# Attention and MLP in fp32 on one core: the MLP as two groups of four batches, with 26 products of sums for each matrix product

## The chip, the core and the metric

The kernel runs on one core of one Trainium2 chip. The core has five engines with instruction streams of their own: TensorE (PE in the profile, with its weight loads as PEld), VectorE (DVE), ScalarE (ACT), GpSimd (POOL, unused here) and SyncE (SP), which issues all transfers between DRAM and the on-chip memory SBUF; 16 DMA engines carry them out. PE writes its results to PSUM, from where DVE or ACT takes them. The metric is the device time of one execution in microseconds. Before the change it was 1048.71 us, the median of three runs from 1046.14 to 1048.9.

## The reference

Sigmoid attention over 8 batches with 12 heads of 448 rows and 64 columns, and behind it an MLP over all 3,584 rows, all in fp32:

```python
scores = scale * np.matmul(q, k.transpose(0, 1, 3, 2)) - np.log(S)
attn = 1.0 / (1.0 + np.exp(-scores))
attn_out = np.matmul(attn, v)                      # 8 x 12 x 448 x 64
x = attn_out.transpose(0, 2, 1, 3).reshape(B * S, H * D)   # 3584 x 768
h = x @ w_in                                       # 768 x 2048
g = h * (1.0 / (1.0 + np.exp(-1.702 * h)))
out = g @ w_out                                    # 2048 x 768
```

The MLP's weights arrive in double precision and are decoded to fp32 on the chip.

## The kernel before

**Precision.** An fp32 operand of the MLP is split into a rounded part and the rest. A matrix product of two operands is three matmuls (high x low, low x high, high x high), added up in PSUM (`TERMS`, function `matmuls`, L819). A split is a rounding copy on ACT or DVE (hi) and a subtraction on DVE (lo): L782, L783 and L785 for weights, L1033, L1034 and L1045 for x and g.

**Attention.** For each pair of heads: scores on PE (L598, L614 for the rows that are left over), a sigmoid on ACT (L584), the product with v on PE (L629, L642), a copy to SBUF (L666, L667) and a store to DRAM (`spill`, named xd). Meanwhile the 16 weight blocks are decoded, DVE and ACT taking turns (L504 to L527), and some of them are stored to DRAM (f).

**MLP.** The 3,584 rows are cut into seven blocks of 512 (`T`). Block 0 is computed directly (`first_block`): 576 matmuls. The other six are two triples (`triple`). For a triple, w_in is 8 blocks (4 x 2) and x is 6 blocks (2 x 3), and in place of the 24 products of blocks it forms 20 products of *sums* of weight blocks with *sums* of x blocks (`W_SUMS`, `X_SUMS`), from which the 12 blocks of h are added up (`H_SUMS`); the same for w_out, g and the output (`G_SUMS`, `O_SUMS`). One product is 36 matmuls in four parts (three parts in the second layer); its result fills four (three) banks of PSUM, and two such places, h0 and h1, take turns. The result is copied (L1178, L1179) or added (L1212) into SBUF, or a later product adds onto it in PSUM (chains, and seeds, which ACT copies into PSUM first, L1135 and L1137).

Sums of weights are formed once (L762; `sums_ahead` and, in the first triple, `w_sums`), split, and stored split in DRAM (c). Later uses load them from there (w<-c). A weight sum has two halves (h = 0 and 1), each a tile of 768 KB, and the ring `wsplit` has four of these tiles. Splits of x or g lie in the ring `pair`, which has two.

**What sets the order.** `Plan.run` places all tasks by a list of keys and estimated costs, and writes each engine's stream in that order. PE's order in the MLP is `SEQUENCES`. Streams are in order: an instruction that waits holds up all behind it on its engine, on SP as well. Buffers for sums are slots of three sizes (`SLOTS`), some of which open only when attention has ended (`LATE_SLOTS`).

Of the kernel before, what the change touches and what calls it, by code (L numbers as in the profile page):

```python
# [20 lines left out]
T = 512  # L21
# [16 lines left out]
ATTENTION, LATE = ("qk", "vraw", "a", "al", "raw64", "e", "qkraw", "x32"), ("wsplit",)  # L38
# [44 lines left out]
class Apart:  # L83
# [216 lines left out]
class Sums:  # L300


    def __init__(self, ops, uses, leaf, cost, make, fresh):
        self.ops = {o[0]: o[1:] for o in ops}
        self.leaf, self.cost, self.make, self.fresh = leaf, cost, make, fresh
        self.left, self.nodes = {}, {}
        for _, a, b, _ in ops:
            for v in (a, b):
                self.left[v] = self.left.get(v, 0) + 1
        for v in uses:  # L310
            self.left[v] = self.left.get(v, 0) + 1

    def get(self, v):
        if v in self.nodes:
            return self.nodes[v]
        if v not in self.ops:
            self.nodes[v] = self.leaf(v)
            return self.nodes[v]
# [15 lines left out]
        self.nodes[v] = Node(into, view, [t])  # L334
        return self.nodes[v]
# [3 lines left out]
def sigmoid_attention_mlp(ctx: ExitStack, tc: tile.TileContext, qk, v, w, out):  # L339
# [62 lines left out]
    def make(b, tag, shape, dtype, name):  # L402
        late = tag in LATE or tag == b.slot and int(tag[1:]) >= EARLY_SLOTS[tag[0]]
# [11 lines left out]
        if b.apart:  # L415
            psum[tag].close()
            banks("z", "left" if tag == "h0" else "right")
            b.tile = Apart([
                spaces["z"].tile([P, T], dtype, tag=f"z{i}", name=f"{name}_{i}", bufs=1) for i in range(NJ)
            ])  # L420
            return b.tile
# [31 lines left out]
    def round_and_rest(costs, b, src, deps, uses, hi, lo, first=lambda: None):  # L453
# [7 lines left out]
        else:  # L461
# [13 lines left out]
    combined = [[[dram.tile([P, 2 * NW_EL], F32, name=f"c{m}_{r}_{h}", tag=f"c{m}_{r}_{h}") for h in range(2)]  # L475
                 for r in range(len(PRODUCTS))] for m in range(2)]
# [4 lines left out]
    def decode(n):  # L481
# [48 lines left out]
        decoded[n] = [Node(f, held(f, f"w32_{n}", NW_EL, k * NW_EL), [t_p]) for k in range(2)]  # L530
        if n >= NW // 4:
# [3 lines left out]
    xs = {}  # L535
# [113 lines left out]
    def places(b):  # L649

        cut = (T - S) * b
        if cut:
            yield b - 1, slice(T - cut, T), slice(0, cut)
        if cut < S:
            yield b, slice(0, S - cut), slice(cut, S)

    copies = []

    def to_x(b, p, t, ps):
# [9 lines left out]
        for block, into, cols in places(b):  # L669
            for js in ([slice(0, 2)] if p % NJ < NJ - 1 else [slice(0, 1), slice(1, 2)]):  # L670
                k, j = divmod(p + js.start, NJ)
                n = js.stop - js.start
                d = dma(lambda block=block, into=into, k=k, j=j, n=n: spill[block][k][:, j : j + n, into],
                        lambda cols=cols, js=js: xb.tile[:, js, cols], n * P * (cols.stop - cols.start) * 4 / 1024, [c], [xb])
                for i in range(n):
                    spilled.setdefault((block, p + js.start + i), []).append(d)

    def make_x(block, k):
        x = buffer("pair")
        n = NJ * T  # L680

        def first():
            if x.tile is None:
                make(x, "pair", [P, 2, 4, T], F32R, f"x{block}_{k}")

        t = [dma(lambda j=j: x.tile[:, 1, j].bitcast(F32), lambda j=j: spill[block][k][:, j], P * T * 4 / 1024,
                 spilled[block, k * NJ + j], [x], first) for j in range(NJ)]
        xs[block, k] = (round_and_rest(
            (act(n), cast(n), dve(n)), x, lambda: x.tile[:, 1, :NJ].bitcast(F32), t, [],
            lambda: x.tile[:, 0, :NJ], lambda: x.tile[:, 1, :NJ],  # L690
        ), x)

# [65 lines left out]
    FULL, PIECE, XB, GB = slice(0, N2), NW_EL, NJ * T, 4 * T  # L758
# [17 lines left out]
    def used_as(block):  # L776
        return [r for r, v in enumerate(W_USES) if v == block]
# [549 lines left out]
```

## Time and profile before

| What | Value |
|---|---|
| Three runs | 1048.9, 1048.71, 1046.14 us |
| The profiled execution | 1047.47 us, its span 1045.5 us |
| Granted TensorE clock | 1.00 |
| HBM | 185.60 MB read, 84.93 MB written |
| DMA queue of SP | 114,640 packets, 270.57 MB, 74.0% of 16 engines |
| L819, first layer's products (p<-xp,w) | 1,440 matmuls, 328.6 us busy |
| L819, second layer's products (p<-gp,w) | 1,440 matmuls, 328.6 us busy |
| L819, block 0 (h<-x,w and o_q<-g,w) | 576 matmuls, 133.0 us busy |

The span is the time from the first to the last instruction on the core; the execution's time is a little longer. Busy times of an engine are united, so overlapping instructions count once. Names in a row are tiles, output first: xp and gp are split sums of x and g, w a split weight block or sum, p a product in PSUM, h and o sums of products, c and f weights in DRAM.

### The profile page before, as it was taken

The numbers are of one execution on the slowest core, as the hardware profiler recorded it, in microseconds if no ns is written. First come the engines' busy times: TensorE is split into PE (matmuls) and PEld (weight loads), VectorE is DVE, ScalarE is ACT, GpSimd is POOL, SyncE is SP. The second block draws the span as 40 slices with busy tenths as digits, with TensorE's granted clock in tenths as the row PEclk, the third lists the DMA queues.
The fourth block names the chain that finished last, engine by engine and source line by source line (L and its number), as shares of the span: only waits on it lengthen the run. The fifth ranks groups of instructions, "written<-read, shape, count | busy, mean of one in ns | idle before, by whom it ended". The sixth has DMA issues, their size and how long they took to land.

```text
span 1045.5 us, 13568 instructions
## 1 busy us (share of the span) xinstructions
PE 1036.4 (99%) x5300; PEld 779.4 (75%) x5300; DVE 852.2 (82%) x758; ACT 543.0 (52%) x497; POOL 0.2 (0%) x4
## 2 busy tenths in 40 slices
PE   9999999999999999999999999999999999999998
PEld 5545555555888877888887888888888888788886
DVE  6999999882998758788998989999874596888685
ACT  6878888875655432533554444333443263534342
POOL 0000000000000000000000000000000000000000
PEclk9999999999999999999999999999999999999999
DMA  9999998973999998756656666859766545454666
GB/s 348 371 362 395 336 397 297 324 258 127 345 332 369 363 377 299 254 193 225 212 170 227 223 210 189 294 200 368 273 232 199 192 139 192 135 167 152 213 201 219
DMA packets 114703, 271.43 MB, mean 260 GB/s; under 512 B 10320, under 2 KB 80080, under 8 KB 112592
## 3 DMA queue, kind: packets, MB, share of 16 engines
q1 hardware_dynamic: 114640, 270.57, 74.0%
q8 instruction: 42, 0.69, 0.3%
q14 instruction: 21, 0.17, 0.0%
HBM read 185.60 MB, written 84.93 MB: 259 GB/s over the span
## 4 chain that ended last, share of the span: by engine, by line
PE 90%; DVE 4%; DMA 2%; ACT 2%; issue 1%; SPq 0%; DVEq 0%; ACTq 0%
PE p L819 55%; PE av L629 11%; PE sc L598 9%; PE h L819 6%; PE o_q L819 5%; PE sc L614 2%; PE av L642 2%; DMA w<-c 1%; DVE gp L1045 1%; DVE h L762 1%; ACT gp L1033 1%; ACT o L1178 1%; DVE o L1179 1%; DMA qkraw<-qk 0%; DVE gs L762 0%
## 5 line engine op out<-in xcount | busy, mean ns | idle before, releaser
L819 PE MATMUL p<-xp,w 128*128 128x512 f32 x1440 | 328.6, 389 | 2.9 <-DMA w<-c 1.2
L819 PE MATMUL p<-gp,w 128*128 128x512 f32 x1440 | 328.6, 389 | 1.1 <-DVE gp L1045 1.1
L819 PEld LDWEIGHTS p<-xp,w 128*128 128x128 f32 x1440 | 270.0, 188 | 60.4 <-issue 2.3
L819 PEld LDWEIGHTS p<-gp,w 128*128 128x128 f32 x1440 | 270.0, 188 | 58.4 <-DVE gp L1045 1.9
L584 ACT ACTIVATE a<-sc,bias 128x896 f32<-128x896 f32 x168 | 156.1, 1017 | 46.1 <-PE sc L614 30.2
L629 PE MATMUL av<-a,vraw 128*64 128x448 f32 x576 | 113.5, 543 | 0.0
L598 PEld LDWEIGHTS sc<-qk 64*128 64x128 f32 x846 | 75.8, 184 | 26.7 <-PE sc L614 16.2
L598 PE MATMUL sc<-qk 64*128 64x448 f32 x846 | 94.3, 373 | 0.3 <-DVE qk L469 0.3
L629 PEld LDWEIGHTS av<-a,vraw 128*64 128x64 f32 x576 | 39.2, 137 | 63.2 <-issue 45.5
L1178 ACT COPY h<-p 128x2048 f32<-128x2048 f32 x18 | 33.7, 1874 | 91.4 <-PE p L819 62.0
L1045 DVE TENSOR_TENSOR gp<-h,gp 128x2048 fp32r<-128x2048 f32 x31 | 70.9, 2288 | 9.1 <-ACT gp L1033 8.7
L1033 ACT CAST gp<-h 128x2048 fp32r<-128x2048 f32 x23 | 44.0, 1912 | 44.8 <-PE p L819 37.5
L819 PE MATMUL h<-x,w 128*128 128x512 f32 x288 | 66.6, 389 | 0.0
L819 PE MATMUL o_q<-g,w 128*128 128x512 f32 x288 | 66.4, 389 | 0.0
L1212 DVE TENSOR_TENSOR h<-h,p 128x2048 f32<-128x2048 f32 x23 | 52.1, 2284 | 17.5 <-PE p L819 10.3
L819 PEld LDWEIGHTS h<-x,w 128*128 128x128 f32 x288 | 54.0, 188 | 11.9 <-issue 0.7
L819 PEld LDWEIGHTS o_q<-g,w 128*128 128x128 f32 x288 | 54.1, 188 | 11.2
L1178 ACT COPY o<-p 128x1536 f32<-128x1536 f32 x18 | 25.9, 1443 | 59.6 <-PE p L819 19.2
L762 DVE TENSOR_TENSOR h<-h,h 128x2048 f32<-128x2048 f32 x24 | 54.7, 2285 | 0.1
L782 ACT CAST wc<-ws 128x384 fp32r<-128x384 f32 (+1 forms) x51 | 28.3, 582 | 47.0 <-DVE ws L762 23.7
L1045 DVE TENSOR_TENSOR xp<-x,xp 128x1536 fp32r<-128x1536 f32 x22 | 38.6, 1754 | 16.6 <-ACT xp L1033 16.5
L1033 ACT CAST xp<-x 128x1536 fp32r<-128x1536 f32 x19 | 28.1, 1481 | 43.6 <-PE p L819 31.5
(108 smaller groups left out, 984.8 us busy)
## 6 DMA issues: line engine op xcount, KB each, us to landing
w<-c SPq DMA_DIRECT2D x140, 384.0 KB, 4.2
w<-c SPq DMA_DIRECT2D x52, 768.0 KB, 4.7
w<-w SPq DMA_DIRECT2D x16, 1536.0 KB, 9.7
c<-wc SPq DMA_DIRECT2D x56, 384.0 KB, 5.3
qkraw<-qk SPq DMA_DIRECT2D x47, 448.0 KB, 6.9
vraw<-v SPq DMA_DIRECT2D x24, 448.0 KB, 8.4
c<-wc SPq DMA_DIRECT2D x14, 768.0 KB, 4.9
c<-w SPq DMA_DIRECT2D x28, 384.0 KB, 4.2
```

The lines of the kernel that those rows point to most:

```text
L584: nc.scalar.activation(a.tile, ps.tile[:, :, :S], AF.Sigmoid, bias=bias, scale=scale)
L598: nc.tensor.matmul(ps.tile[:, j, :S], lhsT=src[kk][rows, S + c * P : S + (c + 1) * P], rhs=src[qq][rows, :S], start=i == 0, stop=i == len( ...
L614: nc.tensor.matmul(ps.tile[cols, j, :S], lhsT=src.tile[rows, S + NC * P :], rhs=src.tile[rows, :S], start=True, stop=True, skip_group_chec ...
L629: nc.tensor.matmul(ps.tile[cols, n % 2, :S], lhsT=vr.tile[:, at : at + D], rhs=a.tile[:, j], start=c == 0, stop=False, skip_group_check=True,)
L642: nc.tensor.matmul(ps.tile[cols, k, :S], lhsT=vr.tile[rows, at : at + D], rhs=a.tile[rows, j], start=False, stop=True, skip_group_check=True,)
L762: return task("DVE", cost, lambda: nc.vector.tensor_tensor(out(), x(), y(), op=op), deps, uses)
L782: t_hi = on_either((act(n), lambda: nc.scalar.copy(into()[:, 0], node.view())), (cast(n), lambda: nc.vector.tensor_copy(into()[:, 0], node ...
L819: nc.tensor.matmul(ps, lhsT=ws[:, a, c * P : (c + 1) * P], rhs=x[:, d, k], start=start and i == 0 and j == 0, stop=stop and i == len(todo) ...
L1033: t_hi = on_either((act(n), lambda: nc.scalar.copy(part(0)(), node.view())), (cast(n), lambda: nc.vector.tensor_copy(part(0)(), node.view())),
L1045: nc.vector.tensor_tensor(part(1)(), node.view(), part(0)().bitcast(F32), op=ALU.subtract)
L1178: t = on_either((act(self.n), lambda: nc.scalar.copy(view(), node.view())), (dve(self.n), lambda: nc.vector.tensor_copy(view(), node.view())),
L1212: nc.vector.tensor_tensor(view(), x.view(), y.view(), op=ALU.add if s0 == s else ALU.subtract)
```

## The change

T becomes 448, so that a block of rows is a batch. The MLP is two groups of four batches (`ROWS = 4`); `first_block` and `triple` go. For a group, w_in is 8 blocks and x is 8 (2 x 4), and the 32 products of blocks are 26 products of sums; likewise in the second layer. There are 104 products of 36 matmuls of 448 columns. New tables say which sums; they have 18 sums of weights (14 before), 18 of x (12), 28 of g (16). One list, `SEQUENCE`, orders the products of both groups and layers; its entries are (group, layer, product).

A weight block is whole now, 1536 columns, and a split one is one tile of 1536 KB in the ring `raw64`, which has two and which the decoding uses earlier; `wsplit` goes. A weight sum is made at its first use, split and stored split (c), and later uses load it.

New is `Sums.used` with `KEEP_FOR`: a sum (or a block) whose next use is further off in the sequence than its number says goes back to DRAM (kw, kx, kg; blocks of x and w_out are there already) and is loaded again. All blocks of g of group 0 are stored when they are made (`AWAY_G`) and loaded for their uses (gl).

```diff
-T = 512
+T = 448
+ROWS = 4
...
-    pair=2, wsplit=4, q0=1, q1=1, q2=1, q3=1, h0=1, h1=1, z=1,
+    pair=2, q0=1, q1=1, q2=1, q3=1, h0=1, h1=1, z=1,
 )
-SLOTS = dict(s=1536, g=2048, t=384)
-EARLY_SLOTS, LATE_SLOTS = dict(s=7, g=4, t=0), dict(s=0, g=9, t=13)
+SLOTS = dict(s=1536, g=1792)
+EARLY_SLOTS, LATE_SLOTS = dict(s=12, g=0), dict(s=2, g=12)
...
+AWAY_G = (0,)
+
+SEQUENCE = (
+    (0, 0, 12), (0, 0, 18), (0, 0, 8), (0, 0, 17), (0, 0, 6), (0, 0, 9), (0, 0, 24), (0, 0, 25),
...
+KEEP_FOR = dict(
+    w0={1: 3, 3: 6, 5: 3, 7: 6, 8: 3, 9: 6, 10: 6, 11: 6, 12: 25, 13: 6, 14: 3, 16: 12, 17: 25, 19: 3, 20: 3, 21: 3, 22: 12, 23: 3, 24: 25, 25: 3},
...
+    def used(self, v):
+
+        turns = self.turns[v]
+        turns.pop(0)
+        if self.left[v] > 0 and turns and turns[0] - self.now > self.keep_for.get(v, math.inf):
+            node = self.nodes.pop(v)
+            if v not in self.back:
+                self.back[v] = self.put(v, node)
...
-    FULL, PIECE, XB, GB = slice(0, N2), NW_EL, NJ * T, 4 * T
+    PIECE, XB, GB = N2, NJ * T, 4 * T
...
     def weights_ring(name):
-        b = buffer("wsplit")
+        b = buffer("raw64")
...
+        def kept(self, name, shape, node, kind):
+
+            kb = P * math.prod(shape) * 4 / 1024
+            n = math.prod(shape)
+            at = dram.tile([P, *shape], F32, name=name, tag=name)
+            t = dma(lambda: at, node.view, kb, node.done, [node.b])
+            node.readers.append(t)
+            count = [0]
+
+            def again():
+                b = plan.slot(kind)
+                count[0] += 1
+                view = tiled(b, f"{name}_{count[0]}", n)
+                return Node(b, view, [dma(view, lambda: at, kb, [t], [b])])
+
+            return again
...
+        def piece_of(self, q, m, r):
+            v = W_USES[r]
+            self.w_later[m, v] -= 1
+            self.begun.add((m, v))
+            b, into, first = weights_ring(f"w{m}_{q}_{r}")
+            if (m, v) in self.saved:
+                t = dma(lambda: into().bitcast(F32), in_dram(m, v), 4 * KB, [self.saved[m, v]], [b], first)
+            else:
+                sums = self.w[m]
+                node = sums.get(v)
+                sums.left[v] -= W_USES.count(v)
                 t = split_piece(node, PIECE, into, b, first)
+                sums.used(v)
+                if self.w_later[m, v]:
+                    self.saved[m, v] = dma(in_dram(m, v), lambda: into().bitcast(F32), 4 * KB, [t], [b])
+            return t, b, into
...
             for i in range(parts):
+                todo = [(i * NJ + j, j) for j in range(NJ)] if m == 0 else [(c * NJ + i, c) for c in range(4)]
...
+                    matmuls(ps.tile[:, i, :T], weights(), xb.tile, todo, not more, True)
+
+                t = task("PE", 3 * len(todo) * 0.2, emit, [t_x, t_w, *edge], [ps, xb, wb])
```

What this does to the streams is seen at three places. On PE, where attention ends and the MLP begins, before stood the direct products of block 0 (h and o_q in PSUM, x and g split whole, w a half block; nine or six matmuls a row):

```order
L642 MATMUL av46_2689<-a47_3_2633,vraw7_4_2558 64x448 x4
L819 MATMUL h0_0_2712<-x0_0_773,w0_0_0_0_1564 128x512 x9
L819 MATMUL h0_0_2712<-x0_1_934,w0_0_0_1_1588 128x512 x9
L819 MATMUL h0_0_2712<-x0_0_773,w0_0_0_0_1564 128x512 x9
L819 MATMUL h0_0_2712<-x0_1_934,w0_0_0_1_1588 128x512 x9
L819 MATMUL h0_1_2769<-x0_0_773,w0_0_1_0_2747 128x512 x9
```

and now stand products of sums at once (xp0 a sum of group 0's x, w0 of w_in):

```order
L689 MATMUL av46_2679<-a47_3_2615,vraw7_4_2529 64x448 x4
L829 MATMUL p0_0_12_2718<-xp0_15_2682,w0_0_12_2617 128x448 x36
L829 MATMUL p0_0_18_2767<-xp0_4_2700,w0_0_18_2463 128x448 x36
L829 MATMUL p0_0_8_2828<-xp0_11_2813,w0_0_8_2777 128x448 x36
L829 MATMUL p0_0_18_2767<-xp0_17_2855,w0_0_17_2840 128x448 x36
L829 MATMUL p0_0_6_2932<-xp0_10_2908,w0_0_6_2906 128x448 x36
```

Block 0 is gone from PE, and the first product of sums has moved up to the end of attention.

On DVE, in the second layer of the first triple, these rows stood before, which serve the products with gp1_2, gp1_27 and gp1_25 (gp is a split of g, h and gs are sums, o is a result copied, w a half of a product's weights):

```order
L785 TENSOR_TENSOR w1_1_2_1_5344<-wr1_6_5263,w1_1_2_1_5344 128x384
L1045 TENSOR_TENSOR gp1_2_5347<-h1_2_4015,gp1_2_5347 128x2048
L762 TENSOR_TENSOR gs1_3_5380<-h1_0_5209,h1_7_4822 128x2048
L1179 COPY o1_21_5395<-p1_1_10_5326 128x1536
L1045 TENSOR_TENSOR gp1_27_5397<-h1_11_4075,gp1_27_5397 128x2048
L783 CAST w1_1_19_1_5401<-w1_1_19_1_5401 128x768
L785 TENSOR_TENSOR w1_1_19_0_5399<-w1_1_19_0_5399 128x768
L785 TENSOR_TENSOR w1_1_19_1_5401<-w1_1_19_1_5401 128x768
L762 TENSOR_TENSOR h1_1_3894<-gs1_3_5380,h1_1_3894 128x2048
L1034 CAST gp1_25_5453<-h1_1_3894 128x2048
L1045 TENSOR_TENSOR gp1_25_5453<-h1_1_3894,gp1_25_5453 128x2048
```

and now, in the second layer of group 1, for the three products with gp1_16, gp1_10 and gp1_41 (kg and kw sums that come back from DRAM, wf a block loaded again):

```order
L1218 TENSOR_TENSOR h1_1_5249<-h1_1_5249,p0_1_16_5539 128x1792
L1218 TENSOR_TENSOR h1_2_4698<-h1_2_4698,p0_1_16_5539 128x1792
L806 TENSOR_TENSOR w1_1_22_5599<-ws1_5_5535,w1_1_22_5599 128x1536
L1012 TENSOR_TENSOR gp1_16_5603<-gs1_5_5447,gp1_16_5603 128x1792
L804 CAST w1_1_25_5638<-ws1_4_5062 128x1536
L806 TENSOR_TENSOR w1_1_25_5638<-ws1_4_5062,w1_1_25_5638 128x1536
L1012 TENSOR_TENSOR gp1_10_5653<-kg1_10_1_5504,gp1_10_5653 128x1792
L784 TENSOR_TENSOR ws1_6_5686<-wf9_4873,kw1_9_1_5537 128x1536
L784 TENSOR_TENSOR gs1_6_5689<-h1_1_5249,h1_2_4698 128x1792
L804 CAST w1_1_16_5707<-ws1_6_5686 128x1536
L1014 SCALAR_TENSOR_TENSOR gp1_41_5705<-gs1_6_5689,gp1_41_5705 128x1792
L806 TENSOR_TENSOR w1_1_16_5707<-ws1_6_5686,w1_1_16_5707 128x1536
```

Weights are split in one row of 1536 columns instead of two of 768, sums of weights stand among the products, and adds of products from the first layer (p0) still stand among the splits of the second.

On SP, where weights that were stored split come back, before (each product's weights in two or three transfers, the second one of a row marked x2):

```order
L437 DMA w0_4_18_0_6020<-c0_18_0_149 128x1536
L437 DMA w0_4_18_1_6022<-c0_18_1_150 128x2x384 x2
L437 DMA x4_5_6038<-xd6_1_222 128x1536
L437 DMA out<-o1_4_5594 128x3x512
L437 DMA w0_4_19_0_6070<-c0_19_0_151 128x1536
L437 DMA w0_4_19_1_6072<-c0_19_1_152 128x1536
```

and now, one transfer a product:

```order
L483 DMA w0_1_11_4168<-c0_3_115 128x3072
L483 DMA w0_1_6_4201<-c0_8_119 128x3072
L483 DMA g0_2_195<-h0_2_3763 128x1792
L483 DMA w0_1_17_4247<-c0_13_124 128x3072
L483 DMA g0_7_200<-h0_7_2800 128x1792
L483 DMA g0_1_194<-h0_1_3956 128x1792
L483 DMA w0_1_8_4314<-c0_22_133 128x3072
L483 DMA x1_1_4337<-xd5_0_187 128x1344
L483 DMA w0_1_18_4354<-c0_5_117 128x3072
```

The stores of group 0's g and the loads of x stand between the reloads, and SP takes them in this order.

More of the change, by code (lines that the diff above doesn't have):

```diff
@@ L333, in get, with meet, need @@
         y.readers.append(t)
-        self.nodes[v] = Node(into, view, [t])
-        return self.nodes[v]
+        made = self.nodes[v] = Node(into, view, [t])
+        self.used(a)
+        self.used(b)
+        return made
+    def meet(self, v, turn):
+        if v in self.ops and v not in self.met:
+            self.met.add(v)
+            for u in self.ops[v][:2]:
+                self.meet(u, turn)
+            for u in self.ops[v][:2]:
+                self.turns.setdefault(u, []).append(turn)
+    def need(self, v, turn):
+        self.meet(v, turn)
+        self.turns.setdefault(v, []).append(turn)
+    def used(self, v):
[5 more added lines that the diff above has]
+                self.back[v] = self.put(v, node)
 @with_exitstack
@@ L418, in make @@
             b.tile = Apart([
-                spaces["z"].tile([P, T], dtype, tag=f"z{i}", name=f"{name}_{i}", bufs=1) for i in range(NJ)
+                spaces["z"].tile([P, 512], dtype, tag=f"z{i}", name=f"{name}_{i}", bufs=1) for i in range(NJ)
             ])
@@ L668, in to_x @@
         copies.append(c)
[L669 to L691, printed above, removed]
+        for js in ([slice(0, 2)] if p % NJ < NJ - 1 else [slice(0, 1), slice(1, 2)]):
+            k, j = divmod(p + js.start, NJ)
+            n = js.stop - js.start
+            d = dma(lambda k=k, j=j, n=n: spill[b][k][:, j : j + n], lambda js=js: xb.tile[:, js],
+                    n * P * S * 4 / 1024, [c], [xb])
+            for i in range(n):
+                spilled.setdefault((b, p + js.start + i), []).append(d)
     firsts = []
@@ L1051, in pair_of, with products @@
             node.readers += [t_hi, t_lo]
[L1052 to L1053 removed]
+            sums.used(v)
+            self.last_pair.clear()
+            self.last_pair[key] = t_lo, b
             return t_lo, b
[L1056 to L1058 removed]
+        def products(self, q, m, r, uses, n, parts, sign, onto, deps):
+            t_w, wb, weights = self.piece_of(q, m, r)
+            t_x, xb = self.pair_of(q, m, uses[r][0], n, f"{'xg'[m]}p{q}_{uses[r][0]}", sign)
@@ L1223, in gelu, with store @@
             node.readers.append(t)
-            g_nodes[i] = Node(b, view, [t])
-        def store(i, sign, node, kind):
-            k, n = divmod(i, 3)
-            into, bank = out[one + n, k * NJ : (k + 1) * NJ].rearrange("j p t -> p j t"), node
+            self.g_nodes[q][i] = Node(b, view, [t])
+            if q in AWAY_G:
+                self.spilled_g[q, i] = dma(lambda: away[q, i], view, P * GB * 4 / 1024, [t], [b])
+        def store(self, net, i, sign, node, kind):
+            q = net.q
+            k, n = divmod(i, ROWS)
+            into, bank = out[q * ROWS + n, k * NJ : (k + 1) * NJ].rearrange("j p t -> p j t"), node
             parts = [slice(0, NJ)]
             if kind == "psum":
-                last = one + 3 == NB and all(left < 0 for left in nets[1].left.values())
+                last = bool(node.apart)
                 parts = [slice(j, j + 1) for j in range(NJ)] if last else parts
-                b, view = nets[1].slot(("out", i))
+                b, view = net.slot(("out", i))
                 node, ends = Node(b, view, []), node.each if last else node.done
@@ L1259, in triple @@
-        sequence = SEQUENCES[one > 1]
-        nets = (Net(0, *H_SUMS, X_SUMS[1], GB, 4, "h", gelu), Net(1, *O_SUMS, G_SUMS[1], XB, NJ, "o", store))
-        places = {}
-        for i, (m, r) in enumerate(sequence):
-            if r in nets[m].chains:
-                onto = places[nets[m].when[nets[m].chains[r][1]]]
-            else:
-                tag = "h1" if turn[0] == "h0" else "h0"
-                onto = buffer(tag), tag
-                onto[0].apart = one + 3 == NB and i == len(sequence) - 1
-            turn[0] = onto[1]
-            places[i] = onto
-            nets[m].product(r, onto)
```

661 lines of the change are left out of this document (282 added, 379 removed), and 12 rows, old and new, of the table SEQUENCE.

## The prediction

> **What bounds the kernel now.** I read the page's head first, cut the span in two with busy times by window, followed the chain of waits, and asked last who waits for whom. In a row of windows stand the stretch, its length, busy us and instructions of PE, PEld, DVE, ACT and POOL, the granted clock, the DMA share and GB/s.
>
> ```profile
> span 1045.5 us, 13568 instructions
> ...
> PE 1036.4 (99%) x5300; PEld 779.4 (75%) x5300; DVE 852.2 (82%) x758; ACT 543.0 (52%) x497; POOL 0.2 (0%) x4
> ```
>
> ```profile
> 252.10:1041.80 789.70, 785.66 (x3456) 648.00 (x3456) 644.81 (x538) 340.29 (x291) 0.00 (x0) 1.00 0.70 238
> 0.00:252.10 252.10, 250.72 (x1845) 131.40 (x1845) 207.39 (x220) 202.12 (x205) 0.20 (x4) 1.00 0.88 327
> ```
>
> PE is busy for 99% of the span. The span has two parts: attention until 252.1 us, then the MLP, whose 3,456 matmuls are just those of the first row. DVE has 644.81 us of work there and the DMA engines are 70% in use; neither is the limit. Whether PE's pitch is steady is read from the chain (start, length, what):
>
> ```profile
> 109.07 3.91 PE sc L598 x36
> ...
> 350.24 8.16 PE o_q L819 x36
> ...
> 376.82 11.56 DMA w<-c
> ...
> 1041.80 0.60 ACT o L1245
> ```
>
> 36 matmuls of 512 columns take 8.16 us, 226.7 ns each. 3,456 are 96 such groups, 783.4 us; the window lasts 789.7, so the MLP loses only 6.3 us to waits. They are small and few:
>
> ```profile
> PE p L819 <- DMA w<-c: 1.2, 2, 0.9
> PE p L819 <- DVE gp L1045: 1.1, 2, 0.9
> ```
>
> So the time before is the columns that PE streams, at one pitch, with 252.1 us of attention ahead and 3.7 us behind (1045.5 less 1041.8). The profiled execution took 1047.47 us, 2.0 outside its span and 1.2 under the median of 1048.71; the sum is made against it. The changed kernel ends the same way, in single parts that are copied and stored, so it keeps 3.7 and 2.0.
>
> **PE.** 3,456 matmuls of 512 columns become 104 products of 36 matmuls of 448 columns, 3,744. The MLP's rows have no 448, but the scores do: 448 columns, a load of 128 weight columns for each, two matmuls at a time on different rows of the array.
>
> ```profile
> 109.30:111.30 2.00, 2.00 (x22) 1.71 (x20) 2.00 (x3) 1.44 (x3) 0.00 (x0) 1.00 1.03 439
> ```
>
> 20 weight loads, ten pairs, in 2.00 us: 200 ns a pair. By columns alone 226.7 x 448/512 gives 198.3, the lower end; the whole score group (3.91 us for 18 pairs) gives 217, but it holds the change from another kind of matmul, which the MLP has not within a product, so it is no end here. I take 200: a product is 7.2 us, all of them 748.8 (742.6 at the lower end) where 783.4 stood. **34.6 us less for PE.** The page TensorE: Matmul & The Clock Gate of the Trainium skill (section Back-to-back issue gap) gives N/2.4 + 2.5 ns for a warm matmul; for 512 that is 215.8, and the trace has 226.7, so the trace decides; for 448 it would be 189.2, and PE's sum 708.
>
> The attention part stays. PE is its limit (250.72 of 252.10), and its DMAs, counted from SP's order, are 78.5 MB, 311 GB/s over 252 us where the row has 327. New there are ten DVE rows at its end (sums and splits for the first two products, about 14 us). DVE has room for them:
>
> ```profile
> 200.00:250.00 50.00, 50.00 (x376) 26.47 (x370) 29.72 (x31) 37.89 (x39) 0.00 (x0) 1.00 0.64 236
> ```
>
> Were they late, the MLP would begin later by as much, at most those 14 us; I take 0.
>
> **DVE.** This is what comes to the limit. Durations are linear in the columns, so 1792 and 1344 lie on the line through these rows:
>
> ```profile
> L1045 DVE TENSOR_TENSOR gp<-h,gp 128x2048 fp32r<-128x2048 f32 x31 | 70.9, 2288 | 9.1 <-ACT gp L1033 8.7
> L1045 DVE TENSOR_TENSOR xp<-x,xp 128x1536 fp32r<-128x1536 f32 x22 | 38.6, 1754 | 16.6 <-ACT xp L1033 16.5
> L1034 DVE CAST gp<-h 128x2048 fp32r<-128x2048 f32 x8 | 9.8, 1225 | 4.1 <-PE p L819 4.0
> L1034 DVE CAST xp<-xs 128x1536 fp32r<-128x1536 f32 x6 | 5.7, 958 | 7.6 <-PE p L819 7.5
> ```
>
> (2288 - 1754)/512 is 1.043 ns a column: 2.021 us at 1792, 1.554 at 1344, 1.754 at 1536; casts 1.091, 0.858, 0.958. Consecutive ones overlap: the MLP's 533 rows of before, each by its group's mean, sum to 672.6 us, and 644.81 were busy, 52 ns less for each. In the order of after I mark DVE's last row for each product and sum between marks. Behind the first product's operands and up to the 40th's stand 71 operations of 1344, 36 of 1536, 44 of 1792 and 19 casts: 279.2, less 170 x 0.052, **270.4 us beside 39 products of PE, 280.8**. Up to the 85th: 92 of 1792, 43 of 1344, 41 of 1536, 9 casts: 333.8 less 9.6, **324.1 beside 45 products, 324.0**. To the last: 127.1 beside 136.8. In all DVE has 721.6 us of work where 644.81 stood, in a shorter time. What fills it: a group has 18 sums of x and 28 of g to form (12 and 16 before), and 26 operands a layer to split instead of 20.
>
> How full can DVE be without PE waiting?
>
> ```profile
> 654.00:738.00 84.00, 84.00 (x372) 69.60 (x371) 79.67 (x53) 28.52 (x22) 0.00 (x0) 1.00 0.83 291
> 374.00:402.00 28.00, 26.10 (x114) 20.71 (x113) 16.75 (x18) 7.18 (x7) 0.00 (x0) 1.00 1.03 399
> 262.00:290.00 28.00, 28.00 (x125) 23.18 (x124) 27.83 (x39) 17.71 (x25) 0.00 (x0) 1.00 0.92 350
> ```
>
> 79.67 of 84 us, 94.8%, and 27.83 of 28, 99.4%, with PE busy throughout both. With 94.8% as DVE's most, the first stretch takes 285.2 (4.4 over PE) and the middle 341.9 (17.9 over): 22 us. With 99.4% only the middle is over, by 2. The first is what DVE was asked for, not its limit, the second is short, so I go between: 97%, which gives the middle 334.1, **10 us of PE waiting**, ends 2 and 22. A wait is dear here, since behind a DVE add that waits for a product stand the splits of the next one, which PE needs.
>
> ACT gets some 20 us more by the same count; with 340.29 busy of 789.70 it has room, and nothing is added for it.
>
> **DMA.** From the first load of group 0, the changed kernel issues 245 transfers: 103 of 1536 KB, 63 of 896, 46 of 672, 27 of 768 and six small, 274.3 MB; before it was 238 GB/s x 789.7 us = 188 MB. At 399 GB/s, reached over 374:402, they take 687 us beside 749. Three places are denser: products 9 to 24 (49.4 MB, 124 us beside 115), 41 to 48 (24.7 MB, 62 beside 58), 73 to 80 (24.3 MB, 61 beside 58), 16 us over together. Part of that is late stores that nobody waits for, part falls where DVE is over anyway: I take **5 us**, ends 0 and 16.
>
> **Sum.** 252.1 + 748.8 + 10 + 5 + 3.7 + 2.0 = **1022 us**, 2.4% less than 1047.5. With the low ends of PE and DVE it is 1002, with all high ends 1045.
>
> **Rivals.**
>
> *PE alone sets it.* The order keeps both queues ahead and almost nothing is lost, as before (6.3 us): 252.1 + 748.8 + 5.7 is 1007, with 6.3 us of waits 1013. For it speaks 262:290, against it that DVE's middle stretch has no slack in 324 us. Chance 0.17.
>
> *Slower: whole weights in a ring of two.* Before, a product's weights came in halves through four buffers; now each is one tile of 1536 KB out of two. A reload can start only when the product two before it has ended, and has one product, 7.2 us, to land. Median times from issue to landing, first over 690:740, then over 740:1040:
>
> ```profile
> w<-c SPq DMA_DIRECT2D x7, 768.0 KB, 7.1
> ```
>
> ```profile
> w<-c SPq DMA_DIRECT2D x19, 768.0 KB, 4.3
> ```
>
> The second half adds 0.79 MB at 399 GB/s, 2.0 us: 6.3 us in the quiet stretch, 9.1 in the busy one (82% DMA share). There are 56 reloads. Each us over 7.2 costs PE 56; the gain of 40.5 (1047.5 less 1007) is gone at a mean of 7.9. At 8.3 the kernel takes 1007 + 62 = 1069. For it speaks that 687 us of transfers in 764 is 90% in use; against it that a reload which PE waits for gives the queue time to drain, and that SP issues mostly one or two transfers between reloads, 2.3 to 4.6 us of them with 896 KB each. Chance 0.13.
>
> *Slower: the DMA engines carry less.* If the MLP's transfers ran at what the MLP of before shows for full use, 238/0.70 = 340 GB/s, they would take 807 us: 252.1 + 807 + 5.7 = 1065. It decides from 347 GB/s down. Against it:
>
> ```profile
> DMA packets 114703, 271.43 MB, mean 260 GB/s; under 512 B 10320, under 2 KB 80080, under 8 KB 112592
> ```
>
> Before, 70% of the packets are under 2 KB; weights in the new layout are rows of 12 KB (3072 columns), and 399 and 439 GB/s stand above. Chance 0.08. The page DMA: Bandwidth & Descriptors of the Trainium skill (Specifications) puts HBM for a core at about 358 GB/s; at that the transfers take 766 us and the kernel at least 1024, close to the forecast. Those two windows ran above it; no run here shows it over 700 us.
>
> That the change does not do what it says is ruled out by the order: 104 products of 36 stand on PE.
>
> **How the numbers follow.** Forecast 0.62, PE alone 0.17, ring 0.13, DMA rate 0.08. About 0.3% is what a measurement of this kernel tells from no change, 3 us. The first gives faster except for its last edge (0.60 of 0.62), the second always, the others in a fifth or less of their cases (0.02 together): faster 0.79, same 0.05, slower 0.16. The range runs from 1008, with a few hundredths of the PE case below it, to 1047, above which are most of the two slow rivals: 0.2 left out. Likeliest: 1022.
>
> **What would show it.** The pitch: 36 matmuls of the chain in 7.2 us (7.14 to 7.2). DVE: over 93% busy in the MLP, and the PE waits led by DVE's splits (xp, gp, w), most of them between the 40th and the 85th product. DMA: share near 0.9 at 350 GB/s or more, and little PE waiting for w<-c. If instead PE waits for w<-c in most reloads, the ring was the price that I set too low; if the share is 1.0 at less than 347 GB/s, the rate; if the MLP begins later than 253 us, the cover at the end of attention was missing.

## The result and the profile after

The changed kernel takes 1088.82 us, the median of four runs (1087.74 to 1088.99), where the kernel before, measured beside it, takes 1048.81. The ratio is 1.0385 with a 95% interval of 1.0367 to 1.0403: **3.9% slower**, where 1022 us and a faster kernel had been forecast. The head of the page and the two parts of the span, which answer to the rows of before:

```profile
span 1087.0 us, 13651 instructions
...
PE 1033.0 (95%) x5588; PEld 836.8 (77%) x5588; DVE 942.3 (87%) x658; ACT 564.6 (52%) x452; POOL 0.2 (0%) x4
```

```profile
0.00:252.50 252.50, 251.10 (x1844) 131.45 (x1845) 217.84 (x226) 199.07 (x203) 0.20 (x4) 1.00 0.89 328
252.50:1083.30 830.80, 781.57 (x3744) 705.31 (x3744) 724.43 (x432) 365.02 (x249) 0.00 (x0) 0.99 0.87 326
```

Attention lasts as long as before (252.5 for 252.1), and 3.4 us follow the MLP's last matmul, which ends at 1083.6 (the window ends 0.3 us before it). All of the difference is in the MLP, 830.8 us where the forecast had 763.8. It issues exactly 3,744 matmuls, and DVE's work in it is 724.43 us (721.6 forecast). But PE, busy for 99% of the span before, stands still between matmuls. Its list of waits (engine, line waited at, what came last, us in total, times, the longest):

```profile
PE p L829 <- DMA w<-c: 31.0, 21, 4.7
PE p L829 <- DVE gp L1012: 6.1, 6, 1.6
PE p L829 <- DVE xp L1012: 5.1, 7, 1.5
PE p L829 <- DVE w L806: 2.4, 2, 1.3
```

The largest wait is for w<-c, the reload of a split weight, not for DVE. A stretch of the chain of waits shows how it recurs (start, length, what):

```profile
424.64 7.55 PE p L829 x36
...
432.62 11.93 DMA c<-w
...
444.62 8.25 DMA w<-c
...
453.01 31.00 PE p L829 x144
...
484.02 7.69 DMA w<-c
...
491.84 7.54 PE p L829 x36
...
499.40 9.90 DMA w<-c
...
509.44 7.55 PE p L829 x36
...
517.00 8.36 DMA w<-c
...
525.50 7.69 PE p L829 x36
```

and later:

```profile
856.16 10.93 DMA c<-w
...
867.15 8.54 DMA w<-c
...
875.82 16.41 PE p L829 x72
```

A product ends, a reload of 7.7 to 9.9 us starts at that moment, and the chain comes back to PE when it has landed; the one product that PE has meanwhile (36 matmuls at 203.9 ns, 7.3 us) is not long enough to cover it. In the trace 54 of the 56 reloads are issued 0.02 us after the end of the product that held their tile. The other two come behind the *store* of a freshly split weight that holds the tile (c<-w, 11.93 us at 432.62 and 10.93 us at 856.16); they cause the two longest waits, 4.4 and 4.7 us of the 31.0. Issues of the whole kernel (transfers, KB each, median us from issue to landing):

```profile
w<-c SPq DMA_DIRECT2D x56, 1536.0 KB, 7.7
c<-w SPq DMA_DIRECT2D x48, 1536.0 KB, 6.9
```

The excess of the MLP can be split by the starts of the 3,744 matmuls in the trace. 3,605 of the 3,743 distances are under 250 ns and average 203.9; at that pitch the MLP would last 763 us. The other 138 add 67.7 us: 54.6 in 37 waits of over 0.7 us, 13.1 in 101 distances of 0.25 to 0.7. Such a sum is called "gaps" below; nearly half of it here is waits for w<-c.

### The profile page after: what moved, and what is told of

Read it like the earlier page. It is cut to its first block, busy times and chain, and to the rows that moved or that the text cites. A ratio compares the mean times of both kernels' runs of the same rounds, so it can differ in the third digit from the quotient of the medians.

```text
span 1087.0 us, 13651 instructions
## 1 busy us (share of the span) xinstructions
PE 1033.0 (95%) x5588; PEld 836.8 (77%) x5588; DVE 942.3 (87%) x658; ACT 564.6 (52%) x452; POOL 0.2 (0%) x4
## 4 chain that ended last, share of the span: by engine, by line
PE 65%; DMA 18%; DVE 11%; issue 4%; ACT 2%; SPq 0%; DVEq 0%; ACTq 0%
PE p L829 43%; DMA w<-c 13%; PE av L676 9%; PE sc L645 8%; DMA c<-w 3%; DVE h L1218 2%; DVE w L806 2%; PE sc L661 2%; DVE gp L1012 2%; PE av L689 2%; DVE xp L1012 1%; ACT h L1184 1%; DVE gs L784 1%; DMA kw<-ws 1%; DMA kw<-w 1%
## 5 line engine op out<-in xcount | busy, mean ns | idle before, releaser
L829 PE MATMUL p<-gp,w 128*128 128x448 f32 x1872 | 392.2, 370 | 26.6 <-DMA w<-c 17.4
L829 PE MATMUL p<-xp,w 128*128 128x448 f32 x1872 | 390.5, 369 | 22.9 <-DMA w<-c 13.6
L829 PEld LDWEIGHTS p<-gp,w 128*128 128x128 f32 x1872 | 353.3, 190 | 65.2 <-issue 23.7
L829 PEld LDWEIGHTS p<-xp,w 128*128 128x128 f32 x1872 | 352.1, 189 | 61.2 <-issue 21.4
L1184 ACT COPY h<-p 128x1792 f32<-128x1792 f32 x38 | 62.7, 1657 | 107.3 <-PE p L829 78.2
L645 PEld LDWEIGHTS sc<-qk 64*128 64x128 f32 x846 | 75.8, 184 | 26.5 <-PE sc L661 16.2
L1218 DVE TENSOR_TENSOR h<-h,p 128x1792 f32<-128x1792 f32 x39 | 77.7, 2018 | 13.2 <-ACT h L1184 9.0
L1045 ACT ACTIVATE h<-h 128x1792 f32<-128x1792 f32 x31 | 52.2, 1700 | 15.4 <-DVE h L1218 15.4
L515 DVE TENSOR_TENSOR qk<-qkraw,qk 128x896 fp32r<-128x896 f32 x47 | 50.6, 1088 | 0.6
L1012 DVE TENSOR_TENSOR gp<-gl,gp 128x1792 fp32r<-128x1792 f32 x19 | 38.4, 2023 | 11.6 <-ACT gp L1000 11.5
L1218 DVE TENSOR_TENSOR o<-o,p 128x1344 f32<-128x1344 f32 x27 | 41.6, 1550 | 5.0 <-PE p L829 5.0
L1012 DVE TENSOR_TENSOR xp<-x,xp 128x1344 fp32r<-128x1344 f32 x26 | 40.4, 1553 | 3.9 <-ACT xp L1000 3.9
L803 ACT CAST w<-ws 128x1536 fp32r<-128x1536 f32 x17 | 25.2, 1480 | 35.5 <-PE p L829 29.6
```

Of the source, the lines that this page charges most:

```text
L515: lambda: nc.vector.tensor_tensor(lo(), src(), hi().bitcast(F32), op=ALU.subtract),
L645: nc.tensor.matmul(ps.tile[:, j, :S], lhsT=src[kk][rows, S + c * P : S + (c + 1) * P], rhs=src[qq][rows, :S], start=i == 0, stop=i == len( ...
L803: t_hi = on_either((act(n), lambda: nc.scalar.copy(into()[:, 0], node.view())), (cast(n), lambda: nc.vector.tensor_copy(into()[:, 0], node ...
L829: nc.tensor.matmul(ps, lhsT=ws[:, a, c * P : (c + 1) * P], rhs=x[:, d, k], start=start and i == 0 and j == 0, stop=stop and i == len(todo) ...
L1012: nc.vector.tensor_tensor(part(1)(), node.view(), part(0)().bitcast(F32), op=ALU.subtract)
L1045: t = task("ACT", act(GB), lambda: nc.scalar.activation(view(), node.view(), AF.Gelu_apprx_sigmoid, scale=float(sign)), [*node.done, *(nod ...
```

## The experiments

The theory was the **ring**: with two whole tiles, a reload can only begin when the product before the last has given its tile back, and must land within one product. Its rivals were DVE's load, the rate of the DMA engines, the place of the reloads in SyncE's queue, and a pitch that is set by the load of weights. The before kernel ran beside each run, at a median between 1047.7 and 1049.0.

### 1. Reloads in halves, the planner told of it

A reload becomes two transfers, one for each half of the columns, and the matmuls use one half after the other; the planner has a ring for each half.

```diff
-t = dma(lambda: into().bitcast(F32), in_dram(m, v), 4 * KB, [self.saved[m, v]], [b], first)
+t = [dma(lambda h=h: into()[:, :, h].bitcast(F32), lambda h=h: in_dram(m, v)()[:, :, h], 2 * KB,
+         [self.saved[m, v]], [half], first)
+     for h, half in zip((slice(0, HALF), slice(HALF, PIECE)), b)]
```

> The changed kernel, with each reload of split weights as two transfers of 768 KB, one for each half of the columns, into the same two tiles; a product's matmuls use one half and then the other (the second net takes its contraction blocks 0 and 1 for all three banks, then 2 and 3), so a half is free half a product earlier. Bytes, tiles, sums and matmuls are as many as in the changed kernel. Ring theory (PE waits because a reload of 7.7 us must fit between one product's end and the start of the next but one, 7.4 us): a half then has 11 us for its way, PE's waits for w<-c fall from 31.0 us to under 8, the slow matmuls behind them go too, and the time to 1035-1055. DVE theory (VectorE's sums bound the stage): waits move to sums, time above 1075. DMA-throughput theory (269.9 MB in the stage are too much): no change, 1080-1090, with a DMA share near 1.0 where PE waits.

Measured: 1104.41 us, 1.0533 of before (1.0505 to 1.0561), slower than the change itself. The waits at PE:

```profile
PE p L835 <- issue: 16.1, 4, 6.0
PE p L835 <- DVE gp L1020: 9.4, 7, 2.0
PE p L835 <- DMA w<-c: 9.1, 7, 3.8
PE p L835 <- ACT h L1193: 8.4, 1, 8.4
```

The waits for w<-c fell as the ring theory said, from 31.0 to 9.1 us. But the planner had written new orders for VectorE, ScalarE and SyncE, and other waits came. (The 16.1 us under "issue" are waits for which the profile shows no cause; they stay open.) The longest single one, 8.4 us, in the chain of waits:

```profile
559.71 1.71 ACT h L1054
561.43 7.75 DMA g<-h
569.26 1.66 ACT h L1193
570.97 32.16 PE p L835 x144
```

A bank copy (L1193) waits until a result of the first layer has been stored to DRAM and its slot is free, and PE waits for the bank. The run changed two things, the halves and the order, so it settles nothing about the first.

### 2 to 4. Half the bytes, half of DVE's sums, fewer columns

Three runs that keep the changed kernel's order row for row.

```diff
-t = dma(lambda: into().bitcast(F32), in_dram(m, v), 4 * KB, ...)
+t = dma(lambda: whole()[:, 0].bitcast(F32), lambda: in_dram(m, v)()[:, 0], 4 * KB, ...)
+into = lambda: High(whole())
```

> The changed kernel, but each of the 56 reloads brings the high half of the pair alone (768 KB instead of 1536 KB), and the products of reloaded weights use the high part where the low part stood: the low part of reloaded weights is left out of the computation. Order and number of all instructions stay. Ring theory: a reload lands in about 5 us, inside a product's 7.4 us; waits for w<-c fall below 8 us, time 1035-1055, and about the same as with the halves, which move all bytes. DMA-throughput theory: 43 MB less, some 110 us of transfer time less, time well under that of the halves. DVE theory: above 1075.

Measured: **1057.47 us** (ratio 1.0092, 1.0063 to 1.0120), 31 us less than the changed kernel. The reload lands in 5.0 us, and PE's waits for it shrink to one:

```profile
w<-c SPq DMA_DIRECT2D x56, 768.0 KB, 5.0
```

```profile
PE p L839 <- DMA w<-c: 0.8, 1, 0.8
```

```diff
+part = slice(0, (n // T + 1) // 2 if b is acc.b or b is node.b else None)
-nc.vector.tensor_tensor(view(), x.view(), y.view(), op=...)
+nc.vector.tensor_tensor(view()[:, part], x.view()[:, part], y.view()[:, part], op=...)
```

> The changed kernel with VectorE's in-place sums of product results done on half of the banks only (the other half of those sums is left out of the computation): same order and instruction count, about 80 us less work for VectorE. DVE theory: most of the 67 us that the stage runs over its forecast goes, time under 1045. Ring theory: VectorE's own waits and part of the late stores of split weights go, at most 17 us: 1070-1085, with PE's waits for w<-c at 25 us or more.

Measured: 1078.57 us (1.0298, 1.0273 to 1.0323). The edit took 76 us of work from DVE (648.64 busy where 724.43 was, over 252.5 to 1083), and only 10 came off the time; the waits for w<-c are as long as before:

```profile
PE p L829 <- DMA w<-c: 30.4, 25, 4.7
PE p L829 <- DVE xp L1012: 2.4, 6, 0.5
```

So DVE's load is not the main thing that holds the changed kernel.

```diff
+n = T if (i, j) in ((0, 0), (len(todo) - 1, 2)) else 384
-    ps, lhsT=..., rhs=x[:, d, k], ...
+    ps[:, :n], lhsT=..., rhs=x[:, d, k, :n], ...
```

> A measurement of the pitch, not of the time: in each group of three to four blocks the first and the last matmul run over 448 columns and those between over 384 (columns 384 to 447 are left out of most products). If a 448-column matmul's pitch of 203.8 ns is set by the stream of columns, the pitch falls in proportion or to about 174 ns (a time 60 us or more lower unless the ring holds it); if it is set by the load of the next weights (188 ns each), it stays at 200-204 ns and the time at 1085-1090.

Measured in one run: 1067.23 us. In a product without waits, 37 matmul records take 6.40 us here and 7.30 in the changed kernel (in a row of windows for one line: length, PE, PEld, clock, DMA share, GB/s):

```profile
792.90:799.30 6.40, 6.40 (x37) 6.20 (x36) 1.00 0.76 273
```

```profile
723.40:730.70 7.30, 7.30 (x37) 6.76 (x37) 1.00 0.85 355
```

2,882 distances average 174.3 ns, while the record of a weight load still lasts 188 ns there, so the load does not set the pitch: columns do. From 384 to 512 columns (226.7 ns before) that is 0.41 ns a column and some 17 ns besides, which gives 200.5 at 448. It also shows the ring from the other side. The matmuls had some 89 us less to stream (3,016 of 384 columns, 29.6 ns less each), but a product is now 6.4 us, and the waits for w<-c grow to fill it:

```profile
PE p L830 <- DMA w<-c: 53.8, 34, 6.2
```

### 5. Reloads in halves, the order kept

The planner sees one reload as before; at its place two transfers are issued, and the second layer's matmuls go over contraction blocks 0 and 1 for all banks, then 2 and 3.

```diff
+def reload():
+    first()
+    for h in (slice(0, PIECE // 2), slice(PIECE // 2, PIECE)):
+        nc.sync.dma_start(out=into()[:, :, h].bitcast(F32), in_=in_dram(m, v)()[:, :, h])
+
+t = task("SP", 4 * KB, reload, [self.saved[m, v]], [b])
```

> The first experiment again, but with the orders of VectorE, ScalarE and SyncE of the changed kernel kept as they are: each reload is two transfers of 768 KB at the place of the one, and the matmuls of a product of the second net go over contraction blocks 0 and 1 for all banks before 2 and 3. Ring theory: waits for w<-c fall from 31.0 us to 10 or less as they did in the first experiment, nothing takes their place, and the time is 1050-1062 (the run with half the bytes gave 1057). If the halves themselves cost (twice the transfers, shorter pieces, banks that finish late), as the first experiment's 1104 might say, 1080 or more.

Measured: **1062.34 us** (1.0144, 1.0127 to 1.0161), 26.5 us less than the changed kernel with all of its bytes, sums and matmuls. PE's waits now:

```profile
PE p L829 <- DVE gp L1017: 7.7, 6, 2.0
PE p L829 <- DVE xp L1017: 6.2, 9, 1.5
...
PE p L829 <- DMA w<-c: 2.2, 4, 0.7
```

```profile
252.50:1056.00 803.50, 776.58 (x3746) 702.55 (x3743) 724.30 (x433) 365.67 (x249) 0.00 (x0) 1.00 0.91 336
```

The gaps fall from 67.7 to 38.4 us. The DMA engines carry the same bytes in less time, 336 GB/s where 326 stood, so their rate was not the bound either: run 2, with 44 MB less to move, was only 4.9 us better than this one. Against run 1 it differs in the order alone (which for DVE, ACT and SP is the changed kernel's; PE's is the same in both but for the parts of the last product): the planner's other order costs 42 us.

### 6 and 7. The reloads on a queue of their own

```diff
-t = dma(lambda: into().bitcast(F32), in_dram(m, v), 4 * KB, [self.saved[m, v]], [b], first)
+def reload():
+    first()
+    nc.gpsimd.dma_start(out=into().bitcast(F32), in_=in_dram(m, v)())
+
+t = task("SP", 4 * KB, reload, [self.saved[m, v]], [b])
```

> The changed kernel with its 56 reloads issued by GpSimd in place of SyncE, in the same order, whole, into the same two tiles. Pure ring theory: a reload starts when PE gives the tile back in either case, no change, 1080-1092, w<-c waits 25-35 us. Queue theory (SyncE issues the reload late, because it waits 221 us for splits and 43 us for stores that stand ahead in its queue): w<-c waits fall under 15 us and the time to 1055-1070. A third way: issuing from GpSimd takes longer for each transfer, then waits rise and the time is above 1095.

The other run makes the same change in run 5:

```diff
-        nc.sync.dma_start(out=into()[:, :, h].bitcast(F32), in_=in_dram(m, v)()[:, :, h])
+        nc.gpsimd.dma_start(out=into()[:, :, h].bitcast(F32), in_=in_dram(m, v)()[:, :, h])
```

> Both: reloads as two halves, issued by GpSimd, VectorE's and ScalarE's order of the changed kernel. If ring and queue each hold part of the reloads back, under the better of the two alone by 5 us or more, 1040-1055; if the ring alone does, as the halves with the same order; if the issue by GpSimd is slow, above them.

Measured: 1134.97 us (1.0842, 1.0820 to 1.0864) with whole tiles, 1067.71 (1.0200, 1.0174 to 1.0225) with halves. In the first, PE waits longer for reloads, not shorter:

```profile
PE p L829 <- DMA w<-c: 49.8, 29, 5.2
```

The expectation's third way came true: the time is above 1095. SyncE's queue does not make the reloads late; in the changed kernel it stands at nearly every reload and waits for PE to give a tile back, which is the ring (SyncE's queue, waits as above):

```profile
SPq L483 <- PE p L829: 304.5, 54, 9.2
```

Run 6's trace shows what changed for a reload: from the end of the product that frees its tile to its landing it takes 8.8 us in the mean where the changed kernel has 7.8. Of that 1.0 us, 0.34 passes before GpSimd's issue begins (0.36 us behind the product's end, 0.02 with SyncE), and the rest after it. 56 such reloads are 57 us, and the run is 46 us longer. Why a transfer lands later from that queue was not tried out. Halves take back 67 us.

### 8 to 12. What is left once the ring is open, and whether it can be won

All five stand on run 5. In run 8, DVE's in-place sums are halved by the edit of run 3.

> The fifth experiment (halves, order kept) with VectorE's in-place sums of product results on half of the banks (the other half of those sums is left out of the computation): what VectorE still costs once the ring is open. Of the 38 us by which the gaps between matmuls exceed the pitch there, some 21 stand at VectorE's results. If VectorE is the next bound, they go and slower clock after them with it: 1038-1048. If the ring's end has left something else (ScalarE, SyncE's queue, the clock), 1055 or more.

Measured: 1046.22 us (0.9976, 0.9963 to 0.9988), 16 us under run 5 where the same edit had given 10 with the ring closed. It leaves half of those sums out, so it is a measurement and no better kernel. PE's waits for DVE fall from 21.3 us in run 5 to 7.7, those for w<-c rise to 6.4:

```profile
PE p L829 <- DMA w<-c: 6.4, 5, 2.3
PE p L829 <- DVE xp L1017: 3.1, 7, 1.3
PE p L829 <- DVE gp L1017: 2.9, 4, 1.6
PE p L829 <- DVE h L1232: 1.7, 1, 1.7
```

```diff
-t = task("PE", 36 / parts * 0.2, emit, ...)
+t = task("PE", 36 / parts * 0.2045, emit, ...)
```

> The fifth experiment with the planner's price of a matmul at 204.5 ns in place of 200, so that it orders the other engines for the pace that TensorE has on the chip. Bytes and instructions stay, the orders change. If the order decides little, 1055-1070; if it decides as much as between the first and the fifth experiment (42 us), anything from 1040 to 1100. The ring theory asks only that PE's waits for w<-c stay below 12 us in any case.

Measured: 1074.31 us (1.0249, 1.0228 to 1.0270), 12 more than run 5. The waits for w<-c stay small (2.6 us); DVE's grow. The order again, by an input that hardly changed.

```diff
+eng = nc.gpsimd if cost == dve(PIECE) else nc.vector
-return task("DVE", cost, lambda: nc.vector.tensor_tensor(out(), x(), y(), op=op), deps, uses)
+return task("DVE", cost, lambda: eng.tensor_tensor(out(), x(), y(), op=op), deps, uses)
```

> The fifth experiment with the sums of weights (36 instructions of about 1.76 us, some 60 us of VectorE's work) computed by GpSimd, which is idle, in the place that the order gives them. If VectorE's load is the next bound and GpSimd does not hinder it, waits for its results fall by a third or more: 1045-1058. If sums on GpSimd take much longer than 1.76 us or slow VectorE, the splits that need them come late: 1065 or more.

Measured: 1121.94 us (1.0701, 1.0681 to 1.0721). A sum of 1536 columns takes GpSimd 4.5 us in the mean of all 36 (4.35 for the seven of this row) where DVE takes 1.75:

```profile
L785 POOL TENSOR_TENSOR ws<-wf,ws 128x1536 f32<-128x1536 f32 x7 | 30.4, 4348 | 37.6 <-DVE gs L785 15.6 <-DVE h L785 11.4 <-DVE w L807 8.9
```

And it can hold DVE up meanwhile. The splits of one line of code in this run, then in run 5 (least, median and greatest ns):

```profile
L807 DVE TENSOR_TENSOR w<-ws,w x22: 1744/1751/5069, 255.5 to 887.9; 128x1536 fp32r<-128x1536 f32 x22
```

```profile
L806 DVE TENSOR_TENSOR w<-ws,w x21: 1747/1749/1759, 265.3 to 829.0; 128x1536 fp32r<-128x1536 f32 x21
```

27 of DVE's operations from 252 us on took over 2.6 us, and all of them ran beside a sum on GpSimd; in run 5 none took so long. Not every operation beside one suffered: the nine adds there that take a product from PSUM kept their time (1.55 or 2.0 us). Of the 60 us lost to run 5, 10 lie ahead of the MLP, which begins at 262.9 us here and at 253.2 there.

```diff
+if mlp:
+    dve = dve[0], act[1]
```

> The fifth experiment with the 49 rounding casts and bank copies of the MLP that the planner gave to VectorE (some 53 us there) emitted for ScalarE in place, at the same point of the order; ScalarE is busy for 366 of 804 us. If VectorE's load is what still bounds, as the eighth experiment says (80 us of load less gave 16 us), 1048-1058; if it is the length of the chain from a bank to the next operand, which a cast on ScalarE makes longer (1.3-1.7 us for 0.9-1.1), 1062 or more.

```diff
+if mlp:
+    return either({"ACT": act[0]}, {"ACT": emit(act[1])}, deps, uses)
```

> The same casts and copies offered to ScalarE alone when the planner sets the order, so that it fits the other work around them. If load bounds, as the run before or up to 8 us under it; if the planner's new order puts reloads or sums late as in the first and ninth experiments, 1070 or more. The ring theory asks for waits for w<-c below 12 us in both.

Measured: 1069.44 us (1.0214, 1.0190 to 1.0239) and 1079.15 (1.0294, 1.0267 to 1.0322), both slower than run 5, though DVE's work fell by 53 us in the first. So DVE's load alone is not the bound. That the longer cast on ACT costs the time, as the expectation supposed, is not shown: in the first of the two PE's waits for DVE's splits are as long as in run 5 (17.3 us for 17.4), and most of what was lost, 5.7 of 6.7 us between the two profiles, is waits for w<-c, 7.9 us for 2.2. What delays these reloads stays open. In the second the longest wait, 8.7 us of 10.7 under "issue", has no cause in the profile. No correct version was found that beats the kernel before.

## Why the prediction was wrong

**The attention part, DVE's work, the end.** Right: 252.5 us for 252.1, 724.4 of work for 721.6, 3.4 behind the MLP for 3.7.

**DMA rate.** Right that it would not bind: a product without waits runs beside 427 GB/s at a share of 1.01,

```profile
716.03:723.30 7.27, 7.27 (x36) 6.75 (x37) 1.00 1.01 427
```

and run 5 moves the same bytes in less time. The sign set for it, 350 GB/s or more, was not met: 326 at a share of 0.87. By the prediction's own way that is 375 GB/s at full use, an estimate, at which the MLP's 271 MB take some 720 us, less than PE's 763. The page DMA: Bandwidth & Descriptors of the Trainium skill (Specifications) has about 358 GB/s of HBM for a core; no run here held more than 341 over its MLP (run 8, 252.75 to 1043.83), but this product ran above it.

**PE's pitch.** A term that was mis-sized: 203.9 ns, not 200, 14.5 us over 3,744 matmuls, so that PE's own gain is 20 us and not 34.6. The score rows from which 200 came are matmuls of 64 rows, two at a time. The line through 384 and 512 columns (run 4) gives 200.5. Of the 3.4 ns above it, 1.2 come from products at a second, slower pitch (below: 202.7 without them, 203.9 with them); the other 2.2 stay open.

**DVE's waits.** In the range: PE waits 16.9 us for DVE's results, with 10 forecast and ends at 2 and 22. But they do not lead PE's waits, they are spread from the first products on instead of gathered in the middle (7.9 us of them between the 40th and the 85th product), and DVE is busy for 87% of the longer MLP, not for over 93%. The 16 us that run 8 takes off show that DVE's results cost more than the 10 forecast once the ring is open.

**Where it failed: the rival "whole weights in a ring of two", with a chance of 0.13.** The sum has no term for PE's waits for reloads; the runs show 31.0 us of such waits in its place, and 26.5 us of time (run 5). The rival's mechanism was right. Its price came out near, in part by luck. It put a us of landing over 7.2 at 56 us; the median landed in 7.7, that is 28 us. But a product lasts 7.3 us; PE waited at 21 of the 56 reloads, not at most of them as the sign for this rival had it; and 9.2 of the 31.0 us are the two waits behind stores of fresh splits, which the rival did not have. Two things were wrong with how it was weighed. First, the argument against it, that a waiting PE gives the queue time to drain: the chain above shows one reload after the other landing in 7.7 to 9.9 us with PE waiting for each. Second, its even point, a mean landing of 7.9 us, was worked out from the full gain of 40.5 us. With the true pitch that gain is 26 and a product 7.34 us, so the even point is 7.8, and the mean landing in the trace is 7.80. The landing that the prediction itself had bounded, 6.3 to 9.1 us, lay on both sides of the 7.2 that were to be had, and a forecast that costs such a thing at nothing had chosen one side.

**The sum.** 67 us lie between forecast and result: 14.5 of pitch, and 67.7 of gaps where 15 were forecast. Opening the ring with all else kept takes 26.5 off (run 5). What remains over the forecast in run 5, 40 us, is the pitch (204.3 there, 16 us) and 23 us of gaps over those forecast; halving DVE's sums takes 16 off again (run 8). So the ring is shown as the largest single cause; without it the change would still have been 1.4% slower here.

## What to carry to other kernels

When a change makes transfers larger and buffers fewer, compare the landing time with the time from one buffer's release to its next use, both from the trace; where they overlap, price it in the forecast itself, for every use, since a stream of in-order products cannot make it up. Splitting such a transfer so that the part that is used first is freed first gave most of the slack back here without more memory. And keep the order fixed when one cause is to be measured: here an order written anew moved the time by 10 to 42 us (run 12 against 11, 9 against 5, 1 against 5) and hid the effect that was looked for.

## What the runs showed of the hardware

A long wait costs PE more than its length. In the changed kernel around the wait that ends at 453.0, 4.80 us from the start of one matmul to the start of the next (length, PE, PEld, clock, share, GB/s):

```profile
441.10:448.20 7.10, 7.10 (x35) 6.59 (x36) 1.00 0.92 347
448.20:453.00 4.80, 0.37 (x2) 0.02 (x1) 1.00 0.95 314
453.00:456.50 3.50, 3.49 (x10) 3.11 (x11) 0.51 1.05 440
456.50:460.00 3.50, 3.50 (x19) 3.25 (x18) 1.00 0.98 356
```

The granted clock is 0.51 for 3.5 us behind it, ten matmuls instead of some 17. In four traces (the change, and runs 1, 5 and 6), no wait of up to 2.1 us, counted from start to start, was followed by more than three slow matmuls (0.25 us or more), while 28 of the 31 from 2.2 us on were followed by 8 to 16 within the next 25. The changed kernel has five such stretches of 3.4 us at half clock, run 5 has two. At 373 ns a matmul instead of 204 each costs some 1.5 us, an estimate, so some 5 of the 26.5 us that run 5 takes off are clock. The page TensorE: Matmul & The Clock Gate of the Trainium skill (HAM oscillation) warns of idle gaps over about 3.4 us; here it begins lower.

The pitch has two values. In products of the changed kernel and of run 5 without waits the distances are either 199 to 207 in a repeating pattern, 202.7 in the mean, or a steady 206.7, for the whole product; which one changes from product to product and from run to run. What chooses it stays open.
